# Fused sparse attention and spectral gate on one core: the POOL queue put in another order, with five smaller moves between engines

## The chip, the cores and the metric

The kernel runs on one core of a Trainium2 chip. A core has a matrix engine (PE, with weight loads shown apart as PEld), a vector engine (DVE), a scalar engine (ACT), a general engine (POOL) and SyncE (SP), which here only issues DMAs. Each engine works through its own instructions strictly in the order in which the program gave them, and waits on semaphores for the others. PE's results land in PSUM, everything else is kept in SBUF. The metric is the device time of one execution in microseconds (us), lower is better; a profiled execution also has a span, from its first to its last instruction.

## What is computed

First comes block-sparse attention: 4 batches of 8 heads, 768 positions, 64 wide, all float32. Each query sees its own block of 64 positions and, of the earlier blocks, those with the three best gate scores (its product with the mean key of a block); causal within that.

```python
k_rep = k.reshape(B, H, n_blocks, block, D).mean(axis=3)
gate_scores = np.einsum('bhsd,bhnd->bhsn', q, k_rep)
...
top_idx = np.argsort(gate_scores, axis=-1)[..., -top_k:]
...
mask = mask & (pos[:, None] >= pos[None, :])
scores = np.where(mask, scores, -1000000000.0)
...
return np.matmul(attn, v).astype(np.float32)
```

The heads of a batch, side by side, are the rows x (768 x 512) of a second stage, which multiplies a long convolution along the sequence with two gates:

```python
proj = x @ w_proj
...
X2 = np.fft.rfft(x2, n=S, axis=1)
H = np.fft.rfft(filter_fft, n=S, axis=0)[None, :, :]
x2_conv = np.fft.irfft(X2 * H, n=S, axis=1)
y = x1 * x2_conv * x3
return (y @ w_out).astype(np.float32)
```

## The kernel before

**Slots.** One loop runs over slots; slot number 3n + s is step s (0, 1, 2) of head n. In step s PE computes one third of head n's transposed scores (`scores`, L404: 4, 3 and 2 matmuls at L409 into a two-bank PSUM tile `sps`), ACT takes the exponential into one of four tiles `ex` (L412), and POOL clears what lies above the diagonal in place (`diagonals`, L415, called triangles below: two operations at L420 in step 0, one in steps 1 and 2). The product with the values follows one slot later (`product`, L426, matmuls L435 into `o`), at the end of PE's work of that slot; `normalise` (L445, DVE) and `turn_outputs` (L454) finish a head or a pair.

**Preparation.** Beside this, `prepare` makes head n+4 ready. In step 0 SP loads keys, queries and values of later heads; DVE casts the queries to fp16 (L306) and subtracts to get their rounding error `rem` (L308); POOL casts the keys (L299) and writes the scaled error (`low_query`, L311). The result `qk` has to be transposed into `qkT`. For heads below 12 (`PE_HEADS`) PE does it in step 2 (`turn_pe`, L329, copies by DVE and ACT at L331); from head 12 on SP issues a transposing DMA in step 1 (`turn_query`, L316). In step 1 of every even head, `gate` (L349 on PE, then DVE up to `gm`, L362) chooses the blocks of heads n+2 and n+3; the choice is transposed and put into `qkT` as 12 more rows, by PE and ACT below head 12 (L378, L380), by two rounds of DMAs on SP after that (`turn_mask`, L368, in step 2, then `place_mask`, L386, in step 0 of the next head). In step 2 POOL casts the values of head n+1 to fp16 (`cast_value`, L335). `prepare_first` has another order for heads 0 and 1, which have no lead of four heads.

**The second stage.** From head 9 on, each slot also holds one or no unit of the batch that has just been completed: X2 (L491, projections and their even and odd parts), F1 (L504, L507: forward transform; DVE multiplies with the filter's spectrum into four tiles `t`), X13 (L530: the two gates), F2 (L543, L546: inverse transform; ACT copies `yes`, DVE makes `yy`) and O (L565: output projection, ACT copies `osb`, SP stores). F1 and F2 stand in step 2 and leave a part for POOL, called in the next slot through the list `todo`: PQ (L519, L520, two subtractions and additions) after F1, yT (L557, L558, two products) after F2. With the plan written in the code these fall into step 0 of heads 11, 12, 13 (PQ) and 14, 15, 16, 17 (yT), and again 8 and 16 heads later; batch 3 follows the last head.

**The setup.** Before head 0, PE, DVE, POOL and ACT build a sine table FS (`phase_mm`, `phase_round`, `phase_turns`, `sines`; the phases are 128 x 384 PSUM tiles, two of them in the two banks of one tile), and head 0 and 1 are prepared; ACT's function table is loaded at its first instruction (L299), for the sines (L218) and for the exponential (L736). The filter is read in two halves `rows`, and in step 2 of heads 3, 4, 5 `filter_rows` turns the order of a block of its second half with a matmul (L624), copies it back on ACT (L625), and makes difference and sum on POOL (L626, L627); step 0 of heads 6, 7, 8 has the filter's spectrum (L635, L638). The weights come through 16 DMAs which POOL issues, 128 KB each (L664), in heads 3 to 13; they convert to fp16.

**What sets the order.** The program is scheduled by hand: the order of the calls in the loop is the order of the instructions on every engine, and nothing reorders them. In a slot it is: scores (with the exponential), normalise, turn_outputs, stores, prepare, diagonals, todo, setup, the unit, product of the slot before:

```python
        if n < NH:
            prepare(n, s)
            diagonals(n, s)
        for fn in todo:
            fn()
```

So in step 0 POOL's queue reads: cast of the keys, `low_query`, two triangles, PQ or yT; in step 2: cast of the values, one triangle.

Of the kernel before, what the change touches and what calls it, by code (L numbers as in the profile page):

```python
# [17 lines left out]
def kernel(  # L18
# [10 lines left out]
    nc = tc.nc  # L29

    B, H, S, D = q.shape
    P = 128
    SC = S // P
    NBLK = S // 64
    Dm = H * D
# [82 lines left out]
    for n in range(3):  # L118
        load_query(n)
        load_key(n)  # L120

# [68 lines left out]
    phases = {}  # L192

    def phase_mm(i):
        if i % 2 == 0:
            phases["big"] = big_tile("dftp")
        pr = phases["big"][:, 512 * (i % 2):512 * (i % 2) + F]
        nc.tensor.matmul(pr, lhsT=tvals[:, P * i:P * (i + 1)], rhs=fsin, start=True, stop=True)
        phases[i] = pr

# [99 lines left out]

    rems = {}

    def split_query(n, copy=nc.vector.tensor_copy):
        qk16 = qk16s[n % NB]
        q_nat = queries.pop(n)
        copy(qk16[:, 0, :, 0:D], q_nat)  # L306
        rems[n] = remp.tile([P, SC, D], FP32, name="rem", tag="rem")
        nc.vector.tensor_sub(rems[n], q_nat, qk16[:, 0, :, 0:D])  # L308

# [22 lines left out]

    def cast_value(n):
        vals[n] = v16s[n % NB]
        nc.gpsimd.tensor_copy(vals[n][:, :, 0:D], values.pop(n))  # L335

    GC = SC - 1

# [282 lines left out]
    def filter_rows(i):  # L621
        fa, fb = rows["all"][:, 0, i], rows["all"][:, 1, HC - 1 - i]
        rev = one_tile("rev")
        nc.tensor.matmul(rev, lhsT=flip, rhs=fb, start=True, stop=True)  # L624
        nc.scalar.copy(fb, rev)  # L625
        nc.gpsimd.tensor_sub(fil[:, 1, i, :], fa, fb)  # L626
        nc.gpsimd.tensor_add(fil[:, 0, i, :], fa, fb)  # L627

    spectra = {}

# [46 lines left out]
    for i in range(HC):  # L677
# [4 lines left out]
        at(7 + i, 0, spectrum_b, i)  # L682
        at(8 + i, 2, inverse_part, i, False)
        at(8 + i, 2, inverse_part, i, True)
    for i in range(DC):
        at(3 + i // 2, 1 + i % 2, weights, wp, moe_w_proj, slice(Dm, 2 * Dm), slice(i, i + 1))
        n = 5 + i
        at(n, 0, weights, wp, moe_w_proj, slice(P * i, P * (i + 1)), slice(0, DC))
        at(n, 1, weights, wp, moe_w_proj, slice(2 * Dm + P * i, 2 * Dm + P * (i + 1)), slice(0, DC))
        at(10 + i, 2, weights, wo, moe_w_out, slice(0, Dm), slice(i, i + 1))  # L690


    nc.vector.memset(lsc, 1.0)
# [27 lines left out]
    key_sums_mm(0, range(SC))  # L721
    small_constants(0)
    small_constants(1)
    turn_pe(0, 1, nc.scalar.copy)
    sines(0)
    key_sums_copy(0)
    key_sums_turn(0)
    turn_pe(0, 0, nc.scalar.copy)
    sines(1)
    key_sums_split(0)  # L730
    sines(2)
    split_query(1, nc.scalar.copy)
    turn_angles()
    nc.scalar.activation(tw, twf, AF.Sin, bias=0.0, scale=math.pi / S)

# [67 lines left out]
    def prepare_first(n, s):  # L803
        if (n, s) == (0, 0):
            gate([1])
            key_mask(2)
            ready_query(2)
            key_sums_mm(2, range(SC))
        elif (n, s) == (0, 1):
            turn_mask_pe([1])  # L810
            key_sums_copy(2)
            key_sums_turn(2)
            key_sums_split(2)
            turn_both(2)
            ready_query(3)
        elif (n, s) == (0, 2):
            turn_both(3)
            for i in range(1, NB):
                nc.gpsimd.memset(v16s[i][:, :, D:DV], 1.0)
            cast_value(1)  # L820
        elif (n, s) == (1, 0):
            gate([2, 3])
            ready_query(4)
        elif (n, s) == (1, 1):
            turn_both(4)
            nc.gpsimd.memset(flip16, 0.0)
            nc.gpsimd.affine_select(
                out=flip16, in_=flip16, compare_op=ALU.not_equal,
                fill=1.0, base=-(P - 1), pattern=[[1, P]], channel_multiplier=1)
            ready_query(5)  # L830
        else:
            turn_mask_pe([2, 3])
            turn_both(5)
            cast_value(2)
# [3 lines left out]
    for slot in range(max(units) + 1):  # L838
        n, s = divmod(slot, 3)
        todo, later = later, []  # L840
        if n < NH:
            if n % H == 0 and s == 0:
                xTs[n // H] = xtp.tile([P, DC, S], fp, name="xT", tag="xT")
            scores(n, s)
            if s == 2:
                scores_left[0] -= 1
        if s == 1 and 0 < n <= NH:
            normalise(n - 1)
        if s == 2 and n % 2 == 0 and 0 < n <= NH:
            turn_outputs(n // 2 - 1, xTs[(n - 1) // H])  # L850
        while stores and stores[0][0] <= slot - (2 if n < NH else 1):
            _, dst, osb = stores.pop(0)
            nc.sync.dma_start(dst, osb)
        if n < NH:
            prepare(n, s)
            diagonals(n, s)
        for fn in todo:
            fn()
        for fn, args in setup.get((n, s), []):
            fn(*args)  # L860
        for b, fn, *args in units.get(slot, []):
            if b not in stages:
                stages[b] = new_stage(b, xTs[b])
            act = fn(stages[b], *args)
            if act is not None:
                later.append(act)

        pn, ps = divmod(slot - 1, 3)
        if 0 <= pn < NH:
            product(pn, ps)  # L870
# [34 lines left out]
```

## Time and profile before

| what | value |
|---|---|
| runs shown | 304.82, 307.81, 309.74 us (median 307.81) |
| profiled execution | 304.75 us, span 303.0 us |
| PE busy (of the span) | 254.1 us (84%) |
| DVE busy | 202.7 us (67%) |
| POOL busy | 174.6 us (58%) |
| ACT busy | 170.7 us (56%) |
| mean granted PE clock | 0.961 |
| the chain that ended last | PE 51%, DVE 17%, POOL 11%, ACT 11%, nothing shown ("issue") 5% |
| start of the first scores | 16.7 us |

Times are counted from the first instruction. Durations below are of the profiled execution, which was the fastest of those shown. A row of the timeline reads: start, duration, engine, line, operation, out <- in, count, and in brackets the engine's idle time before it and what ended that. A row of the waits reads: who waited for whom, us in total, how often, and the longest. Matmuls overlap and their ends are modelled, so busy time of PE is not a measure of its peak.

### The profile page before, as it was taken

The page shows a single profiled execution, that of the slowest core. Times are in us where ns is not written, and L with a number is a line of the kernel's source. Part 1 is how long each engine was busy: PE and PEld are TensorE (multiplying, and loading weights), DVE is VectorE, ACT ScalarE, POOL GpSimd, SP SyncE. Part 2 cuts the span into 40 slices and gives each one's busy share as a digit, 9 for nine tenths or more (in the row PEclk, how much of TensorE's full clock was granted, in tenths as well). Part 3 has the DMA queues.
Part 4 walks back from the last instruction along what each step waited for, and adds up shares of the span by engine and source line. Part 5 has one row for each costly group of instructions (what it writes and reads, how often), then busy time and mean ns, then how long its engine had stood idle before and what let it go on. Part 6 is the DMA issues. An engine that isn't in the chain of part 4 may idle for free.

```text
span 303.0 us, 6290 instructions
## 1 busy us (share of the span) xinstructions
PE 254.1 (84%) x2221; PEld 149.6 (49%) x2221; DVE 202.7 (67%) x597; ACT 170.7 (56%) x254; POOL 174.6 (58%) x330
## 2 busy tenths in 40 slices
PE   5396876766778798888899889997999999999994
PEld 3264564544543355445645454565445565545541
DVE  6566376526898768966766888676588763479740
ACT  3745757365867435454655655576455668632363
POOL 7424557498675229867771386678524866517530
PEclk9999779599999969997999999999999999999999
DMA  9949936833369589898776888799739361000036
GB/s 171 214 90 276 188 80 121 157 45 47 36 78 186 119 148 195 132 201 154 160 148 129 205 160 176 148 206 194 162 77 176 84 94 71 35 35 2 0 144 238
DMA packets 127263, 40.03 MB, mean 132 GB/s; under 512 B 122128, under 2 KB 123392, under 8 KB 127232
## 3 DMA queue, kind: packets, MB, share of 16 engines
q1 hardware_dynamic: 121856, 37.54, 58.9%
q0 software_dynamic: 5376, 2.10, 6.7%
q8 instruction: 17, 0.28, 0.4%
q14 instruction: 14, 0.11, 0.2%
HBM read 24.64 MB, written 6.29 MB: 102 GB/s over the span
## 4 chain that ended last, share of the span: by engine, by line
PE 51%; DVE 17%; POOL 11%; ACT 11%; issue 5%; DMA 2%; SPq 0%; DVEq 0%; ACTq 0%; POOLq 0%
PE sps L409 8%; PE krp L267 7%; PE op L565 5%; PE o L435 5%; ACT ex L412 5%; POOL ex L420 4%; PE x13a L530 4%; PE x13b L530 3%; PE x2b L491 3%; PE x2a L491 3%; DVE rem L308 3%; PE tp L329 2%; POOL qk L311 2%; PE f2b L546 2%; ACT xT L463 2%
## 5 line engine op out<-in xcount | busy, mean ns | idle before, releaser
L412 ACT ACTIVATE ex<-sps 128x1024 f16<-128x1024 f32 (+2 forms) x96 | 87.7, 917 | 76.5 <-PE sps L409 67.9
L420 POOL TENSOR_SCALAR_AFFINE_SELECT ex<-ex 128x128 f16<-128x128 f16 (+1 forms) x128 | 45.0, 363 | 26.6 <-ACT ex L412 24.5
L409 PE MATMUL sps<-qkT 76*128 76x384 f16 (+2 forms) x288 | 55.6, 304 | 0.9 <-DMA qkT<-gmT 0.9
L435 PE MATMUL o<-v,ex 128*128 128x65 f16 x672 | 38.6, 198 | 20.9 <-POOL ex L420 19.1
L311 POOL TENSOR_SCALAR qk<-rem 128x384 f16<-128x384 f32 x32 | 16.8, 526 | 67.9 <-DVE rem L308 59.9
L435 PEld LDWEIGHTS <-ex 128*128 128x128 f16 x672 | 32.6, 100 | 41.3 <-POOL ex L420 26.3
L530 PEld LDWEIGHTS <-wp 128*128 128x128 f16 x256 | 25.1, 99 | 18.0 <-issue 3.5
L267 PE MATMUL krp<-k_nat,eblk 128*12 128x128 f32 (+2 forms) x144 | 28.4, 337 | 1.6 <-DMA k_nat<-in_k_dram 1.6
L409 PEld LDWEIGHTS <-qkT 76*128 76x128 f16 x288 | 21.4, 101 | 6.0 <-issue 1.1
L565 PE MATMUL op<-wo,yT 128*128 128x512 f16 x96 | 23.0, 379 | 0.0
L530 PE MATMUL x13a<-xT,wp 128*128 128x384 f16 x108 | 22.8, 334 | 0.2 <-DVE t L515 0.2
L535 DVE TENSOR_TENSOR gx<-x1sb,x13b 128x384 f32<-128x384 f16 x27 | 14.9, 552 | 12.0 <-ACT x1sb L534 6.5
L530 PE MATMUL x13b<-xT,wp 128*128 128x384 f16 x108 | 22.1, 327 | 0.2
L308 DVE TENSOR_TENSOR rem<-q_nat,qk 128x384 f32<-128x384 f32 x32 | 20.0, 625 | 3.3 <-ACT qk L306 1.0
L558 POOL TENSOR_TENSOR yT<-gx,yy 128x384 f16<-128x384 f32 x16 | 17.2, 1077 | 8.2 <-DVE yy L552 8.2
L519 POOL TENSOR_TENSOR PQ<-t,t 128x512 f16<-128x512 f32 x12 | 15.2, 1265 | 7.5 <-DVE t L512 7.5
L451 DVE TENSOR_TENSOR xn<-o,rz 128x384 f16<-128x384 f32 x32 | 17.8, 557 | 1.1
L329 PE MATMUL tp<-id_f,qk 128*76 128x128 f16 (+1 forms) x144 | 14.1, 252 | 4.4 <-POOL qk L311 2.8
L267 PEld LDWEIGHTS krp<-k_nat,eblk 128*12 128x12 f32 x144 | 11.8, 103 | 12.2 <-issue 4.3
L568 ACT COPY osb<-op 128x512 f32<-128x512 f32 x24 | 14.0, 585 | 6.2 <-PE op L565 5.4
L299 POOL CAST qk<-k_nat 128x384 f16<-128x384 f32 x31 | 16.8, 543 | 0.2
L335 POOL CAST v<-v_nat 128x384 f16<-128x384 f32 x32 | 16.3, 509 | 0.0
(134 smaller groups left out, 472.8 us busy)
## 6 DMA issues: line engine op xcount, KB each, us to landing
q_nat<-in_q_dram SPq DMA_DIRECT2D x32, 192.0 KB
k_nat<-in_k_dram SPq DMA_DIRECT2D x32, 192.0 KB
v_nat<-in_v_dram SPq DMA_DIRECT2D x32, 192.0 KB
out_dram<-osb SPq DMA_DIRECT2D x24, 256.0 KB
rows<-in_moe_filter_fft_dram SPq DMA_DIRECT2D x2, 768.0 KB
wp<-in_moe_w_proj_dram POOLq DMA_DIRECT2D x12, 128.0 KB, 3.5
wo<-in_moe_w_out_dram POOLq DMA_DIRECT2D x4, 128.0 KB, 4.1
qkT<-gmT SPq DMA_DIRECT2D x20, 18.0 KB
```

The source lines that it names most:

```text
L267: nc.tensor.matmul(sums[g][0:NBLK, 0:w * D], lhsT=eblk[:, c, :], rhs=keys[g][:, 0:w, c, :], start=(c == 0), stop=(c == SC - 1))
L308: nc.vector.tensor_sub(rems[n], q_nat, qk16[:, 0, :, 0:D])
L311: nc.gpsimd.tensor_scalar(qk16s[n % NB][:, 0, :, D:P], in0=rems.pop(n), scalar1=LO, scalar2=0.0, op0=ALU.mult, op1=ALU.add)
L329: nc.tensor.transpose(tp[0:rows_, P * c:P * (c + 1)], qk16s[n % NB][:, t, c, 0:rows_], id_f16)
L409: nc.tensor.matmul(sps[:, col:col + qe - qs], lhsT=turned[n][0:76, 1, kc, :], rhs=qT[0:76, qs:qe], start=True, stop=True, skip_group_check ...
L412: nc.scalar.activation(ex[:, lo:hi], sps[:, lo:hi], AF.Exp, bias=0.0, scale=scale)
L420: nc.gpsimd.affine_select(out=sub, in_=sub, compare_op=ALU.is_ge, fill=0.0, base=0, pattern=[[0, cnt], [1, P]], channel_multiplier=-1)
L435: nc.tensor.matmul(outs[n][:, qc * DE:(qc + 1) * DE], lhsT=ex[:, col + P * j:col + P * (j + 1)], rhs=vals[n][:, kc, 0:DE], start=(gi == 0 ...
L451: nc.vector.tensor_tensor(out=xns[n // 2][:, :, D * (n % 2):D * (n % 2 + 1)], in0=o[:, :, 0:D], in1=rz.to_broadcast([P, SC, D]), op=ALU.mult)
L491: nc.tensor.matmul(pp, lhsT=xT[:, dc, base + P * i:base + P * (i + 1)], rhs=wp[:, dc, Dm:2 * Dm], start=(dc == 0), stop=(dc == DC - 1))
L530: nc.tensor.matmul(dst, lhsT=wp[:, dc2, base:base + P], rhs=xT[:, dc2, hs:hs + HALF], start=(dc2 == 0), stop=(dc2 == DC - 1))
L565: nc.tensor.matmul(op, lhsT=yT[:, cc, P * scn:P * (scn + 1)], rhs=wo[:, cc, :], start=(cc == 0), stop=(cc == DC - 1))
```

## The change

Six things change. (1) The loop calls `prepare` after `diagonals` and `todo`, so POOL's queue in a slot holds the triangles first, then PQ or yT, then the casts and `low_query`; the instructions of the other engines keep their order by this, since `diagonals` and `todo` issue only to POOL while heads run. In `prepare_first`, heads 4 and 5 become ready one slot earlier on DVE and POOL (4 in slot (0, 2), 5 in (1, 1) ahead of the flip matrix), and head 4 is transposed in (1, 0). (2) From head 12 on ACT casts the values instead of POOL: 20 of the 32 casts. (3) `filter_rows` has no copy on ACT and nothing on POOL; DVE adds and subtracts straight out of PSUM. (4) The weights come in 8 DMAs of 256 KB in place of 16 of 128 KB. (5) ACT loads the sine table as its first table, so that the load between the first copy and the first sine is gone, and the first copies run under that table; ACT casts head 1's queries before the first sine instead of after the last. (6) The first two phases lie in the first banks of two PSUM tiles, the third in the second bank of the first tile. The program's instructions on PE are the same but for one exchange within slots (1, 0) and (1, 1); ACT has 20 casts more, 3 copies and one table load fewer; DVE has 6 operations more; POOL has 20 casts, 6 filter operations and 8 DMAs fewer, and SP's queue is unchanged.

```diff
--- before.py
+++ after.py
@@ -118,6 +118,7 @@
     for n in range(3):
         load_query(n)
         load_key(n)
+    nc.scalar.preload_act_table_set("trig_and_small")
 
 
 
@@ -192,9 +193,9 @@
     phases = {}
 
     def phase_mm(i):
-        if i % 2 == 0:
-            phases["big"] = big_tile("dftp")
-        pr = phases["big"][:, 512 * (i % 2):512 * (i % 2) + F]
+        if i < 2:
+            phases["big", i] = big_tile("dftp")
+        pr = phases["big", i % 2][:, 512 * (i // 2):512 * (i // 2) + F]
         nc.tensor.matmul(pr, lhsT=tvals[:, P * i:P * (i + 1)], rhs=fsin, start=True, stop=True)
         phases[i] = pr
 
@@ -300,10 +301,19 @@
 
     rems = {}
 
-    def split_query(n, copy=nc.vector.tensor_copy):
+    def split_query(n):
         qk16 = qk16s[n % NB]
         q_nat = queries.pop(n)
-        copy(qk16[:, 0, :, 0:D], q_nat)
+        nc.vector.tensor_copy(qk16[:, 0, :, 0:D], q_nat)
+        query_rest(n, q_nat)
+
+    def cast_query(n, copy):
+        copy(qk16s[n % NB][:, 0, :, 0:D], queries[n])
+
+    def query_rest(n, q_nat=None):
+        if q_nat is None:
+            q_nat = queries.pop(n)
+        qk16 = qk16s[n % NB]
         rems[n] = remp.tile([P, SC, D], FP32, name="rem", tag="rem")
         nc.vector.tensor_sub(rems[n], q_nat, qk16[:, 0, :, 0:D])
 
@@ -332,7 +342,8 @@
 
     def cast_value(n):
         vals[n] = v16s[n % NB]
-        nc.gpsimd.tensor_copy(vals[n][:, :, 0:D], values.pop(n))
+        copy = nc.gpsimd.tensor_copy if n < PE_HEADS else nc.scalar.copy
+        copy(vals[n][:, :, 0:D], values.pop(n))
 
     GC = SC - 1
 
@@ -622,9 +633,8 @@
         fa, fb = rows["all"][:, 0, i], rows["all"][:, 1, HC - 1 - i]
         rev = one_tile("rev")
         nc.tensor.matmul(rev, lhsT=flip, rhs=fb, start=True, stop=True)
-        nc.scalar.copy(fb, rev)
-        nc.gpsimd.tensor_sub(fil[:, 1, i, :], fa, fb)
-        nc.gpsimd.tensor_add(fil[:, 0, i, :], fa, fb)
+        nc.vector.tensor_add(fil[:, 0, i, :], fa, rev)
+        nc.vector.tensor_sub(fil[:, 1, i, :], fa, rev)
 
     spectra = {}
 
@@ -682,12 +692,13 @@
         at(7 + i, 0, spectrum_b, i)
         at(8 + i, 2, inverse_part, i, False)
         at(8 + i, 2, inverse_part, i, True)
-    for i in range(DC):
-        at(3 + i // 2, 1 + i % 2, weights, wp, moe_w_proj, slice(Dm, 2 * Dm), slice(i, i + 1))
-        n = 5 + i
-        at(n, 0, weights, wp, moe_w_proj, slice(P * i, P * (i + 1)), slice(0, DC))
-        at(n, 1, weights, wp, moe_w_proj, slice(2 * Dm + P * i, 2 * Dm + P * (i + 1)), slice(0, DC))
-        at(10 + i, 2, weights, wo, moe_w_out, slice(0, Dm), slice(i, i + 1))
+    for i in range(2):
+        half = slice(2 * i, 2 * i + 2)
+        at(3 + i, 1, weights, wp, moe_w_proj, slice(Dm, 2 * Dm), half)
+        at(5 + i, 0, weights, wp, moe_w_proj, slice(2 * P * i, 2 * P * (i + 1)), slice(0, DC))
+        at(5 + i, 2, weights, wp, moe_w_proj, slice(2 * Dm + 2 * P * i, 2 * Dm + 2 * P * (i + 1)),
+           slice(0, DC))
+        at(10 + i, 2, weights, wo, moe_w_out, slice(0, Dm), half)
 
 
     nc.vector.memset(lsc, 1.0)
@@ -721,15 +732,16 @@
     key_sums_mm(0, range(SC))
     small_constants(0)
     small_constants(1)
+    cast_query(1, nc.scalar.copy)
+    sines(0)
     turn_pe(0, 1, nc.scalar.copy)
-    sines(0)
     key_sums_copy(0)
     key_sums_turn(0)
     turn_pe(0, 0, nc.scalar.copy)
     sines(1)
     key_sums_split(0)
+    query_rest(1)
     sines(2)
-    split_query(1, nc.scalar.copy)
     turn_angles()
     nc.scalar.activation(tw, twf, AF.Sin, bias=0.0, scale=math.pi / S)
 
@@ -810,24 +822,24 @@
             turn_mask_pe([1])
             key_sums_copy(2)
             key_sums_turn(2)
+            turn_both(2)
             key_sums_split(2)
-            turn_both(2)
             ready_query(3)
+            for i in range(1, NB):
+                nc.gpsimd.memset(v16s[i][:, :, D:DV], 1.0)
         elif (n, s) == (0, 2):
             turn_both(3)
-            for i in range(1, NB):
-                nc.gpsimd.memset(v16s[i][:, :, D:DV], 1.0)
+            ready_query(4)
             cast_value(1)
         elif (n, s) == (1, 0):
             gate([2, 3])
-            ready_query(4)
+            turn_both(4)
         elif (n, s) == (1, 1):
-            turn_both(4)
+            ready_query(5)
             nc.gpsimd.memset(flip16, 0.0)
             nc.gpsimd.affine_select(
                 out=flip16, in_=flip16, compare_op=ALU.not_equal,
                 fill=1.0, base=-(P - 1), pattern=[[1, P]], channel_multiplier=1)
-            ready_query(5)
         else:
             turn_mask_pe([2, 3])
             turn_both(5)
@@ -852,10 +864,11 @@
             _, dst, osb = stores.pop(0)
             nc.sync.dma_start(dst, osb)
         if n < NH:
-            prepare(n, s)
             diagonals(n, s)
         for fn in todo:
             fn()
+        if n < NH:
+            prepare(n, s)
         for fn, args in setup.get((n, s), []):
             fn(*args)
         for b, fn, *args in units.get(slot, []):
```

## The prediction

> **What bounds the kernel now.** I read the page first. PE is busiest and heads the chain that ended last, but with half of it; DVE, POOL and ACT hold 39%. So PE is stopped by the others, and the question is where.
>
> ```profile
> PE 254.1 (84%) x2221; PEld 149.6 (49%) x2221; DVE 202.7 (67%) x597; ACT 170.7 (56%) x254; POOL 174.6 (58%) x330
> PEclk9999779599999969997999999999999999999999
> PE 51%; DVE 17%; POOL 11%; ACT 11%; issue 5%; DMA 2%; SPq 0%; DVEq 0%; ACTq 0%; POOLq 0%
> ```
>
> Second, the waits: PE (and its weight loads, in the same stalls) waits above all for POOL's triangles, and POOL above all for DVE's `rem`, although the triangles need no `rem`: `low_query` stands ahead of them in POOL's queue.
>
> ```profile
> POOL qk L311 <- DVE rem L308: 59.9, 24, 6.1
> PEld L435 <- POOL ex L420: 26.3, 24, 4.0
> PE o L435 <- POOL ex L420: 19.1, 16, 3.9
> ```
>
> Third, the timeline at the longest such stall, head 4. The first exponential ended at 50.50 (the merged row covers two).
>
> ```profile
> 49.48 1.83 ACT L412 ACTIVATE ex<-sps 128x1024 f16<-128x1024 f32 x2
> ...
> 50.66 1.38 POOL L627 TENSOR_TENSOR fil<-rows 128x512 f16<-128x512 f32 x1
> 51.02 1.43 DVE L308 TENSOR_TENSOR rem<-q_nat,qk 128x384 f32<-128x384 f32 x1
> 51.98 0.58 POOL L664 DMA_DIRECT2D wp<-in_moe_w_proj_dram  x1
> ...
> 53.17 0.51 POOL L311 TENSOR_SCALAR qk<-rem 128x384 f16<-128x384 f32 x1
> ...
> 53.75 1.01 POOL L420 TENSOR_SCALAR_AFFINE_SELECT ex<-ex 128x256 f16<-128x256 f16 x3
> ...
> 54.57 0.62 PE L435 MATMUL o<-v,ex 128*128 128x65 f16 x8 [3.94 <-POOL ex L420]
> ```
>
> Filter, weight DMA, cast and `low_query` all ran between the exponential and its triangle. Fourth, the same waits by stretch: PE waited for triangles 12.7 us from 16.7 to 111.0 (heads 0 to 10), 4.4 from 111.0 to 163.5, 2.0 after that. The loss is in the first third. Fifth, stretches at half the clock (columns: stretch, length, busy time of PE, PEld, DVE, ACT, POOL, then the clock):
>
> ```profile
> 40.28:43.69 3.41, 3.21 (x32) 2.79 (x30) 2.62 (x13) 2.36 (x4) 1.15 (x3) 0.50 0.51 115
> 53.93:60.76 6.83, 6.14 (x41) 4.19 (x42) 3.06 (x16) 2.95 (x5) 2.46 (x7) 0.50 0.90 173
> 105.13:111.96 6.83, 5.65 (x34) 3.37 (x35) 4.09 (x18) 1.56 (x3) 3.13 (x8) 0.50 0.73 125
> ```
>
> Two more are 30.04 to 33.45 (PE busy 3.27) and 139.27 to 142.68 (3.41). Each came after PE had stood 1.8 us or more: 2.25 at 27.5, 1.95 at 37.6, 3.94 at 50.6, 1.88 at 104.4, 1.80 at 135.3. Stalls of 2.47 at 63.0 and 2.05 at 87.2 had no such sequel, so the link isn't certain.
>
> **The change, part by part**, against the profiled execution (304.75 us, 3.06 below the median of the runs).
>
> *Start: −3.0.* The path was first copy (6.91 to 7.70), table load 1.28, sine, the second phase's addition, which waited 2.92 for that sine, the third, the cast of head 1 on ACT (11.47 to 11.97), `rem` (to 12.57), and only then the gate on DVE (12.48 to 14.53), scores at 16.71. Now: keys 0 are cast by 5.05, queries 1 (landed 5.42) by 5.95, sine 5.97 to 6.46, both copies to 8.66 (0.79 each, the first from 6.91). DVE has done its additions, key splits and `rem` (0.55 + 0.21 + 0.32 + 0.57 + 0.46 + 0.56 + 0.57 from 5.34) by 8.9. The gate starts near 9.1 instead of 12.48, which brings the exponential's table (two sines, 0.21, 1.28) in by 11.2 as the gate ends. That is 3.4 earlier; I take 3.0. Ends: 1.3, the table load's row alone, and 3.4.
> The row has no more than the load: 7.72 + 1.28, sine at 9.02. The Trainium skill, ScalarE: Activation LUTs, section "What ACT_TABLE_LOAD costs", counts a drain of 1380 ns with each switch, 2.66 us in all; by it this part would be 1.4 larger.
>
> *Triangles first, heads 1 to 10: −10.9.* A first triangle (both operations: 0.77) can now end 0.84 after its exponential. Heads 2, 4, 5, 8, 10: exponentials end at 37.42, 50.50, 62.07, 85.87, 103.79, triangles ended at 39.44, 54.51, 65.45, 89.20, 106.25; earlier by 1.18, 3.17, 2.54, 2.49, 1.62. Capped by the stalls (1.95, 3.94, 2.47, 2.05, 1.88) that is 1.18 + 3.17 + 2.47 + 2.05 + 1.62 = 10.49, and 0.39 at head 6.
> *Head 4 earlier: −2.3*, the 2.25 at 27.5 in which PE's transposes waited for `low_query` of head 4. Bounds 0 and 3.5 (with 0.54 and 0.71 at 23.7 and 33.8).
> *Filter on DVE: −1.9*, PE's wait of 1.94 at 69.9 for POOL's L627. DVE gets 6 operations; the nearest rows with an operand in PSUM and the same size are L495 and L496 (686, 679 ns): 4.1 us, hidden where DVE idles (60.0 to 68.6: busy 1.86 of 8.6). Without that cover they delay the next `rem`: at most +4.1.
> *What is late next.* Not all 15.1 stays: the second triangle still stands behind `low_query`, and in step 2 PE's transposes need it. In head 4 the first product ends at 52, scores and half the transposes at 52.8, and `low_query` at 53.2 or later: 0.4 to 1 returns. ACT's mask copies (two of 0.79 a pair) and DVE (14.57 busy in 17.9 from 84.2) come next. I keep two thirds: −10.1. Ends 5 and 15.1.
> *Clock: −4.* PE's 18.3 busy at half clock in the four stretches before 112 would take half at full, 9.1 less at most, 10.9 with the fifth. I take a bit under half, as other stalls remain; at the least 0.
>
> *Triangles first, heads 11 to 27: −3 +5 = +2.* These heads have PQ or yT in step 0. POOL's sum between the exponential and the second triangle is unchanged: 0.77 + 2.51 (PQ) + 0.51 + 0.51 = 4.3. Head 12: exponential ends 119.60, second triangle would end 124.25 instead of 124.40; the 1.05 won at the first product is lost at the second. With yT (1.9 to 2.0) head 14 keeps 1.0 of 1.80. Of 6.4 I keep 3.
> Against it, `low_query` itself comes later, and SP's transposes wait for it:
>
> ```profile
> 115.13 1.42 SPq L316 DMA_TRANSPOSE qkT<-qk  x1
> ...
> 120.18 0.40 PE L349 MATMUL gps<-kr,qkT 128*128 128x24 f16 x10
> ```
>
> In head 11 `low_query` ended at 114.23; now: 113.20 + 0.77 + 2.51 + 1.02 = 117.5. The transpose goes out at 117.5, 2.4 later, and lands (it took 3.84, to 118.97, by the trace's landing records) at 121.4; the gate used it at 120.18. In even heads the late transpose keeps SP from the mask's: head 12's L368 goes from 124.28 to about 125.5, and the mask's landing had 1.0 in hand. Going through all pairs by their slack at the old pace (odd heads 15, 19, 23, 27: 1.9, 1.65, 0.3, 0.8; masks for heads 14 to 30: 0.05 to 4.6) PE waits some 1.2, 0.65, 0.6, 0.3, 0.2 at gates and 2 at scores: 5. Ends 0 and, without slack, 9 odd heads at 2.4 and 8 even ones at 1.2: 31.
> A rule speaks against this order too. Row: `rem` takes 0.56, but 1.43 at 51.02, ending with POOL's L627. The Trainium skill, SBUF — State Buffer, section "SBUF: two separate sides", calls this an exclusive lock: a DVE operation with two SBUF inputs and a POOL operation exclude each other. Triangles used to follow `rem`; now they can meet it, at worst 0.56 in each of some 21 heads, 12 us by that rule.
>
> *Casts on ACT: 0.* 20 at 0.50 (L299 and L306 on ACT: 511, 502 ns), 10 us; ACT waits 67.9 us for PE before exponentials, 17.2 and 26.5 of it in the stretches concerned. Uncovered +10; POOL's 10 us less are a gain only through triangles, at best the 3 above again.
> *Weights: 0.* 16 issues of 0.73 and 0.61, 11.2 us of POOL, become 8; the 4-piece kind took 0.8, so 6.4 at most if the pieces set it (11.2 if bytes do). Triangles in front hide it. Ends −1 and +1.
>
> Sum: −3.0 − 10.1 − 4 + 2 = −15.1, 289.6. Runs scatter from 304.82 to 309.74, above the profiled one; I forecast **290**.
>
> **The rivals.**
> *The transposes become the bound.* For: slack of 0.05 to 1.9, and PE arrives earlier than before. Against: it only hits pairs with PQ or yT, and heads 18 and 26 recover. Without slack +31 against −3 − 10.1 − 4 − 3: 315.6, slower. It decides once the wait exceeds some 3 us for each of nine pairs. 7%.
> *The stall moves.* `low_query` and DVE stop PE in the early heads at another place and the clock stays as it was: −3 − 5 + 2, some 299. For: DVE is busy four fifths of the time from 84 on. Against: its waits for PE there. 15%.
> *ACT is late.* Casts uncovered, +10: 300. For: exponentials queue behind them. Against: the idle time named. 6%.
> *All of it is gained.* −3.0 − 15.1 − 10.9 − 3: 273. For: four of five slow-clock stretches follow a triangle stall. Against: it leaves PE almost no idle time. 10%.
> The forecast, 284 to 297, has 62%.
>
> **How the numbers follow.** The range 277 to 301 leaves out the slower case and the far end of the last. A measurement of this kernel tells about 2% from no change, so faster means below about 301. The forecast and the last case are faster; so is part of the 299 and 300 cases: 0.81. Same 0.10, slower 0.09.
>
> **What would show it.** First scores near 13.5; L311 waiting for `rem` no longer followed by PE's wait for L420 in heads 2 to 10; PE at L635 without a wait; no half clock at 40 and 54; L349 or L409 waiting for DMA `qkT` in heads 12 to 30; L412 not waiting behind casts. It would be wrong if PE's transposes (L329 before) wait for L311 as long as its products did, or if the gates wait more than 3 us a pair.

## The result and the profile after

The changed kernel takes **296.12 us** (median of 4 runs, 294.34 to 297.95); the kernel before, in runs beside it, 307.63. The ratio of times is **0.966, with a 95% interval of 0.956 to 0.975**: faster. The profiled execution of after is its slowest, 297.95 (span 296.2), and that of before its fastest, 304.75, so the traces differ by 6.8 us where the medians differ by 11.5. The four runs of after, 297.95, 296.55, 295.70 and 294.34, had mean clocks of 0.952, 0.965, 0.965 and 0.977: part of the scatter is how many stretches of half clock a run meets.

The page of after, its busy rows, the row of the granted clock, and the shares of the chain that ended last:

```profile
PE 253.3 (86%) x2221; PEld 147.7 (50%) x2221; DVE 201.7 (68%) x603; ACT 175.5 (59%) x270; POOL 160.7 (54%) x296
PEclk9797999999799958999999999978999999999999
PE 51%; DVE 16%; POOL 10%; ACT 8%; DMA 7%; issue 5%; SPq 1%; POOLq 0%; DVEq 0%; ACTq 0%
```

The chain has a little less of POOL and ACT, and DMA has grown from 2% to 7%. The waits of after answer to those of before (us in total, times, longest):

```profile
POOL ex L431 <- ACT ex L423: 93.4, 50, 5.1
...
PEld L446 <- POOL ex L431: 10.0, 15, 1.2
...
PE o L446 <- POOL ex L431: 7.9, 12, 1.1
...
PE sps L420 <- DMA qkT<-gmT: 6.0, 3, 2.9
...
POOL qk L321 <- DVE rem L318: 4.7, 5, 2.2
...
PE gps L360 <- DMA qkT<-qk: 2.9, 3, 1.8
```

POOL's wait for `rem` fell from 59.9 to 4.7 us, and POOL now idles where its triangles wait for ACT's exponentials, which is harmless. PE's wait for triangles fell from 19.1 to 7.9. PE now waits 8.9 us for DMAs into `qkT`, against 0.9 before. The timeline of after at head 4, where the longest stall was:

```profile
43.39 1.83 ACT L423 ACTIVATE ex<-sps 128x1024 f16<-128x1024 f32 x2 [0.89 <-PE sps L420]
...
44.48 0.89 POOL L431 TENSOR_SCALAR_AFFINE_SELECT ex<-ex 128x256 f16<-128x256 f16 x2 [1.34 <-ACT ex L423]
...
45.21 0.57 DVE L318 TENSOR_TENSOR rem<-q_nat,qk 128x384 f32<-128x384 f32 x1
...
45.43 0.42 PE L446 MATMUL o<-v,ex 128*128 128x65 f16 x8 [0.32 <-POOL ex L431]
...
46.24 0.50 POOL L321 TENSOR_SCALAR qk<-rem 128x384 f16<-128x384 f32 x1
```

The triangles start as the first exponential ends, nothing stands between, and the product waits 0.32 us instead of 3.94. Now the same two stretches in both kernels, from the first scores of head 0 to those of head 11, and from there to head 31 (columns: stretch, length, busy time of PE, PEld, DVE, ACT, POOL with the number of instructions, clock, DMA share, GB/s). Before:

```profile
16.71:110.97 94.26, 72.25 (x718) 45.74 (x716) 61.99 (x213) 56.68 (x76) 53.65 (x106) 0.90 0.64 117
110.97:254.60 143.63, 130.25 (x1187) 74.71 (x1184) 104.01 (x302) 84.49 (x128) 92.95 (x172) 0.98 0.78 155
```

After:

```profile
12.96:93.98 81.02, 67.33 (x717) 41.78 (x716) 64.02 (x218) 54.79 (x73) 45.08 (x95) 0.94 0.73 141
93.98:247.78 153.80, 135.28 (x1188) 77.53 (x1185) 101.31 (x303) 92.12 (x148) 88.16 (x152) 0.94 0.71 148
```

This is the whole account. The start is 3.75 shorter (16.71 to 12.96). Heads 0 to 10 lost 13.24: PE idles 13.7 instead of 22.0, and its same matmuls take 67.3 instead of 72.3, since less of them runs at half clock. Heads 11 to 30 gained 10.17: PE idles 18.5 instead of 13.4, and its matmuls take 5.0 longer, at a clock of 0.94 instead of 0.98. From head 31 on nothing changed (48.4 in both). −3.75 − 13.24 + 10.17 is −6.8, the difference of the two profiled executions.

So the early heads gave about what was forecast, and three quarters of it (10.2 of 13.2) were given back later in this trace. PE's waits for `qkT` from DMAs in after, all of them after head 11's start:

```profile
102.76 0.61 PE L420 MATMUL sps<-qkT 76*128 76x128 f16 x4 [1.66 <-DMA qkT<-gmT]
108.45 0.31 PE L360 MATMUL gps<-kr,qkT 128*128 128x24 f16 x5 [1.85 <-DMA qkT<-qk]
136.19 0.61 PE L420 MATMUL sps<-qkT 76*128 76x128 f16 x4 [1.44 <-DMA qkT<-gmT]
169.19 0.29 PE L360 MATMUL gps<-kr,qkT 128*128 128x24 f16 x5 [0.54 <-DMA qkT<-qk]
197.40 1.03 PE L420 MATMUL sps<-qkT 76*128 76x128 f16 x4 [2.90 <-DMA qkT<-gmT]
232.77 0.29 PE L360 MATMUL gps<-kr,qkT 128*128 128x24 f16 x5 [0.52 <-DMA qkT<-qk]
```

Before had one of 0.90. The first two and the 2.90 lie in or just before the two late stretches of half clock:

```profile
103.80:114.04 10.24, 8.39 (x58) 4.77 (x56) 4.81 (x20) 3.95 (x7) 4.78 (x8) 0.50 0.95 183
195.96:202.79 6.83, 5.39 (x33) 3.06 (x34) 2.52 (x7) 2.12 (x3) 3.13 (x5) 0.50 0.77 150
```

### The profile page after: what moved, and what is told of

It reads as the page before. It is cut to its first block, busy times and chain, and to the rows that moved or that the text cites. A ratio compares the mean times of both kernels' runs of the same rounds, so it can differ in the third digit from the quotient of the medians.

```text
span 296.2 us, 6301 instructions
## 1 busy us (share of the span) xinstructions
PE 253.3 (86%) x2221; PEld 147.7 (50%) x2221; DVE 201.7 (68%) x603; ACT 175.5 (59%) x270; POOL 160.7 (54%) x296
## 4 chain that ended last, share of the span: by engine, by line
PE 51%; DVE 16%; POOL 10%; ACT 8%; DMA 7%; issue 5%; SPq 1%; POOLq 0%; DVEq 0%; ACTq 0%
PE sps L420 7%; PE op L576 6%; PE krp L268 6%; DMA qkT<-qk 6%; PE x13b L541 5%; ACT ex L423 4%; PE o L446 4%; PE x2a L502 4%; PE x13a L541 4%; PE x2b L502 3%; POOL ex L431 3%; PE tp L339 2%; PE f1b L518 2%; ACT osb L579 1%; POOL qk L321 1%
## 5 line engine op out<-in xcount | busy, mean ns | idle before, releaser
L423 ACT ACTIVATE ex<-sps 128x1024 f16<-128x1024 f32 (+2 forms) x96 | 87.4, 917 | 67.3 <-PE sps L420 64.1
L431 POOL TENSOR_SCALAR_AFFINE_SELECT ex<-ex 128x128 f16<-128x128 f16 (+1 forms) x128 | 50.4, 408 | 98.3 <-ACT ex L423 93.4
L446 PEld LDWEIGHTS <-ex 128*128 128x128 f16 x672 | 33.0, 99 | 26.0 <-POOL ex L431 10.0
L446 PE MATMUL o<-v,ex 128*128 128x65 f16 x672 | 38.7, 196 | 7.9 <-POOL ex L431 7.9
L268 PE MATMUL krp<-k_nat,eblk 128*12 128x128 f32 (+2 forms) x144 | 27.7, 327 | 1.9 <-POOL dft_ka L210 1.9
L541 PE MATMUL x13b<-xT,wp 128*128 128x384 f16 x108 | 23.3, 341 | 0.5 <-DVE t L526 0.3
L318 DVE TENSOR_TENSOR rem<-q_nat,qk 128x384 f32<-128x384 f32 x32 | 19.1, 598 | 3.2 <-POOL qk L321 0.5
L339 PE MATMUL tp<-id_f,qk 128*76 128x128 f16 (+1 forms) x144 | 13.4, 246 | 5.2 <-POOL qk L321 1.9
L268 PEld LDWEIGHTS krp<-k_nat,eblk 128*12 128x12 f32 x144 | 11.0, 98 | 12.9 <-issue 5.2
L506 DVE TENSOR_TENSOR x2eo<-x2a,x2b 128x512 f16<-128x512 f32 x11 | 7.6, 687 | 11.9 <-PE x2b L502 11.9
```

The lines of the kernel that those rows point to most:

```text
L268: nc.tensor.matmul(sums[g][0:NBLK, 0:w * D], lhsT=eblk[:, c, :], rhs=keys[g][:, 0:w, c, :], start=(c == 0), stop=(c == SC - 1))
L339: nc.tensor.transpose(tp[0:rows_, P * c:P * (c + 1)], qk16s[n % NB][:, t, c, 0:rows_], id_f16)
L423: nc.scalar.activation(ex[:, lo:hi], sps[:, lo:hi], AF.Exp, bias=0.0, scale=scale)
L431: nc.gpsimd.affine_select(out=sub, in_=sub, compare_op=ALU.is_ge, fill=0.0, base=0, pattern=[[0, cnt], [1, P]], channel_multiplier=-1)
L446: nc.tensor.matmul(outs[n][:, qc * DE:(qc + 1) * DE], lhsT=ex[:, col + P * j:col + P * (j + 1)], rhs=vals[n][:, kc, 0:DE], start=(gi == 0 ...
L541: nc.tensor.matmul(dst, lhsT=wp[:, dc2, base:base + P], rhs=xT[:, dc2, hs:hs + HALF], start=(dc2 == 0), stop=(dc2 == DC - 1))
```

## The experiments

Two questions were open. What lengthens the late heads: `low_query` behind PQ and yT, the casts on ACT, or something else? And which part earns the early gain? All diffs are against the changed kernel unless the text says before. The columns: first scores of head 0, heads 0 to 10 (to the first scores of head 11), heads 11 to 30, all from one trace; then the ratio of run times to the kernel before, measured beside it, with its interval; then the range of the run times, with the traced one. No stage times are given for e8, e10 and e11: their traces are of 291.63, 299.08 and 291.91 us, where their runs start at 286.31, 294.02 and 287.32.

| kernel | start | heads 0–10 | heads 11–30 | ratio (95%) | runs, us (traced) |
|---|---|---|---|---|---|
| before | 16.7 | 94.3 | 143.6 | 1 | 304.82–309.74 (304.75) |
| after | 13.0 | 81.0 | 153.8 | 0.966 (0.956–0.975) | 294.34–297.95 (297.95) |
| e1 old order from head 11 | 13.1 | 79.8 | 147.6 | 0.954 (0.950–0.959) | 289.27–291.00 (290.59) |
| e2 casts between triangles and PQ | 12.9 | 81.6 | 144.1 | 0.949 (0.942–0.956) | 287.16–293.19 (288.69) |
| e3 all values cast on POOL | 12.9 | 82.1 | 150.2 | 0.971 (0.962–0.979) | 293.18–296.73 (295.31) |
| e4 before + order alone | 16.6 | 91.8 | 153.6 | 1.019 (1.011–1.027) | 308.55–312.11 (312.11) |
| e5 filter back on ACT and POOL | 13.1 | 86.6 | 150.4 | 0.990 (0.982–0.998) | 300.17–303.63 (300.17) |
| e6 all but the order | 13.1 | 89.8 | 146.1 | 0.972 (0.962–0.982) | 295.57–301.32 (299.15) |
| e7 old start | 16.3 | 79.8 | 150.0 | 0.972 (0.963–0.980) | 296.20–302.54 (296.20) |
| e9 old `prepare_first` | 13.2 | 85.4 | 151.1 | 0.979 (0.971–0.988) | 296.58–299.85 (299.85) |
| e12 before + order, `prepare_first`, filter | 16.5 | 81.3 | 147.9 | 0.978 (0.965–0.990) | 295.82–304.16 (295.82) |

How far apart two traces of the same instructions can lie, the table shows itself. After, e1, e2 and e3 have the same program up to head 10, and take 79.8 to 82.1 there. After, e3, e4, e5, e7, e9 and e12 have the same order in the late heads, and take 147.9 to 153.8 there. So the late loss against before is 4 to 10 us, and the trace of after is at the top of this; differences of 2 us early and of several late tell nothing by themselves.

### The late heads

**e1: from head 11 on, the order of before.**

```diff
         if n < NH:
+            if 11 <= n < NH:
+                prepare(n, s)
             diagonals(n, s)
...
-        if n < NH:
+        if n < 11:
             prepare(n, s)
```

> The changed kernel, but from head 11 on prepare is called ahead of the triangles again, as in the kernel before. Theory A (the late low_query makes PE wait for SP's transposes in heads 11 to 30; the gain is all in the start and heads 1 to 10): PE's waits for DMA at L349 and L409 (9.0 us in the changed kernel) fall below 2 us, heads 11 to 31 take about 152 us instead of 160, and the time is 288 to 291. Rival B (ACT's value casts or the meeting of triangles and DVE's rem cost the time in the later heads, the DMA waits only show it): 294 to 297, since the casts stay on ACT and POOL's waits for rem come back.

Median 290.50. The late heads take 147.6 instead of 153.8, PE's waits for DMA fall from 8.9 to 3.2 us, and the early gain stays. So the order in the late heads is what gives most of the gain back, 6.2 of the 10.2 in these two traces. All its runs are below those of after. Of the 4.0 that stay against before, 2.4 is idle time of PE and 1.6 the clock; the waits at head 12 (below) are 3.0.

**e2: `prepare` between the triangles and PQ or yT, in all heads.**

```diff
         if n < NH:
             diagonals(n, s)
+            prepare(n, s)
         for fn in todo:
             fn()
-        if n < NH:
-            prepare(n, s)
```

> The changed kernel with the order triangles, prepare, todo: the triangles stay first, and the casts and low_query go ahead of PQ and yT. Theory A: low_query ends 2.0 to 2.5 us earlier in heads 11 to 17, 19 to 25 and 27, the DMA waits at L349 and L409 fall from 9.0 to under 3 us, the half clock near 104 and 196 us is gone, and the time is 284 to 290, below the first of these runs, since the triangles keep their place. Rival B: 293 to 297. If PQ and yT, now behind low_query's wait for rem, come late for F2 and O, PE waits at L557 or L576 and the time stays near 296.

Median 289.26, ratio 0.949, 1.8% below the change itself. The two intervals just touch, but no run of e2 (at most 293.19) is as slow as the fastest of after (294.34), so this version beats both kernels. The late heads take 144.1, as in before, with the early gain kept. The wait rows of e2 (whole run):

```profile
PE o L446 <- POOL ex L431: 7.9, 12, 1.1
...
PE sps L420 <- DMA qkT<-gmT: 2.5, 2, 1.7
...
PE gps L360 <- DMA qkT<-qk: 1.3, 1, 1.3
```

The triangles cost PE the same 7.9 as in after; only the DMA waits went. How, is seen at head 22. POOL and SP in the timeline of after (head 22 starts at 181.68, head 23 at 188.08):

```profile
185.49 0.99 POOL L569 TENSOR_TENSOR yT<-gx,yy 128x384 f16<-128x384 f32 x1
...
187.11 0.51 POOL L321 TENSOR_SCALAR qk<-rem 128x384 f16<-128x384 f32 x1
...
187.65 1.43 SPq L326 DMA_TRANSPOSE qkT<-qk  x1
...
190.08 1.26 SPq L379 DMA_TRANSPOSE gmT<-gm  x1
...
193.84 1.96 SPq L397 DMA_DIRECT2D qkT<-gmT  x2
```

and in e2 (starts at 177.81 and 184.19):

```profile
181.22 0.51 POOL L321 TENSOR_SCALAR qk<-rem 128x384 f16<-128x384 f32 x1
...
181.76 1.43 SPq L326 DMA_TRANSPOSE qkT<-qk  x1
...
184.22 1.25 SPq L379 DMA_TRANSPOSE gmT<-gm  x1
...
187.95 1.94 SPq L397 DMA_DIRECT2D qkT<-gmT  x2
```

In after `low_query` ends 5.9 us after its head's start, behind yT; SP's transpose follows at once, the mask's transpose stands behind it in SP's queue, then `place_mask`: 5.76 after the start of head 23. In e2 `low_query` ends at 3.9 and the masks are placed 3.76 after head 23's start, 2.0 sooner. Head 24 needs them: it waits 2.90 in after (197.40), 0.80 in e2.

One pair of waits stayed: at the first scores of head 12 and at its gate, 1.98 and 1.05 in e1, 1.69 and 1.29 in e2, where after has 1.66 and 1.85. There `low_query` isn't the cause. In after it ends at 100.49, but SP is still issuing `place_mask` (99.70 to 101.45), and the transpose goes out at 101.56, 7.58 us after head 11's start. In e2 `low_query` ends 2.46 us closer to the start, and the transpose goes out at 7.60 all the same. From 92 to 103 SP issues with no gap over 0.21, with the two transposes of the filter's tables (L236, L238, 2.5 us) among its work. PE reaches head 11 17.0 us sooner than before (110.97 to 93.98), SP this transpose only 13.6 sooner (115.13 to 101.56).

**e3: all values cast on POOL**, in after; **e8:** the same in e2.

```diff
-        copy = nc.gpsimd.tensor_copy if n < PE_HEADS else nc.scalar.copy
+        copy = nc.gpsimd.tensor_copy
```

> The changed kernel with all values cast on POOL. Theory A: the casts on ACT are hidden and POOL's cast stands in step 2 behind the triangle, where POOL has room: 295 to 298, with the same DMA waits of about 9 us. Rival B (ACT's 20 casts of 0.5 us delay the exponentials): 287 to 292.

> e2_casts_before_pq (289.3: triangles, prepare, PQ or yT) with all values cast on POOL. Theory A (the casts are hidden on ACT, and on POOL they stand behind a triangle in step 2): 288 to 292, no difference that can be told. Rival B (ACT's casts delay exponentials or the copies behind them): 284 to 287, with heads 11 to 31 taking 2 to 4 us less than 144.

e3: 295.57, ratio 0.971 against 0.966 of after; e8: 290.07, 0.939 (0.928 to 0.949) against 0.949 of e2. Neither differs measurably from its partner, and PE's DMA waits in e3 are 6.9. So the casts on ACT are neither a cost nor a gain beyond the 1% or so that the intervals leave open.

**e11: e2 with PQ and yT held back one slot** (all but the last PQ of a batch).

```diff
             diagonals(n, s)
+            prepare(n, s)
+        if s == 0 and n < NH and n % H != 5:
+            todo, later = [], todo
```

> e2_casts_before_pq with PQ and yT held back for one more slot, behind the second triangle, except the last PQ of a batch. Theory A (what PE still loses to triangles in heads 11 to 27 is PQ or yT between the first and the second triangle): waits of PE for L431 after head 11 fall from 5.5 us to under 2, heads 11 to 31 take 140 to 142 us instead of 144, the time is 284 to 288. Rival B (PE waits for something else as soon as it is earlier: masks, transposes, ACT): 288 to 291 with the wait shifted to DMA qkT or ACT.

Median 289.18, ratio 0.948: no different from e2. The waits of e11, in its trace of 291.91 us, say why:

```profile
PE sps L420 <- DMA qkT<-gmT: 6.6, 4, 3.0
...
PE o L446 <- POOL ex L431: 3.3, 5, 1.1
...
PE x13a L541 <- DVE t L526: 1.9, 2, 1.3
...
PE x13b L541 <- DVE t L526: 1.5, 3, 0.8
```

PE's late waits for triangles went from 5.4 us in e2 to 0.8, but waits for placed masks came, 6.6, and 3.4 for DVE's `t`, whose tiles PQ empties. With POOL out of the way the chain of the masks ends last there, as rival B said. That this trace stands for the other runs of e11 isn't shown.

### The early heads

**e4: before, with the new order in the loop and nothing else.**

```diff
--- before
         if n < NH:
-            prepare(n, s)
             diagonals(n, s)
         for fn in todo:
             fn()
+        if n < NH:
+            prepare(n, s)
```

> The kernel before with the loop's order alone (triangles, todo, prepare; nothing else). Theory A: the start stays at 16.7 us, heads 1 to 10 win some 8 us, heads 11 to 31 lose 5 to 8 to waits for transposes: 299 to 306, a small gain or none. Rival B (the order itself is all gain, other parts take it back): 292 to 297.

Both expectations missed: 309.55, ratio 1.019, slower than before. Heads 0 to 10 gain 2.5 (PE idles 3.5 less, its matmuls take 1.0 longer), and the late heads lose 10, as in after. Two things in its trace. First, head 4:

```profile
51.55 1.83 ACT L412 ACTIVATE ex<-sps 128x1024 f16<-128x1024 f32 x2
...
52.74 1.37 POOL L627 TENSOR_TENSOR fil<-rows 128x512 f16<-128x512 f32 x1
...
53.10 1.43 DVE L308 TENSOR_TENSOR rem<-q_nat,qk 128x384 f32<-128x384 f32 x1
...
54.06 0.58 POOL L664 DMA_DIRECT2D wp<-in_moe_w_proj_dram  x1
...
54.65 0.78 POOL L420 TENSOR_SCALAR_AFFINE_SELECT ex<-ex 128x256 f16<-128x256 f16 x2
...
55.48 0.42 PE L435 MATMUL o<-v,ex 128*128 128x65 f16 x8 [2.78 <-POOL ex L420]
```

The cast and `low_query` are gone from the gap, but the filter and the weight DMA of the slot before still stand between exponential and triangle. Second, a stretch at half clock, five times 3.41 us long:

```profile
29.20:46.30 17.10, 14.76 (x122) 10.71 (x123) 9.63 (x42) 9.24 (x12) 7.27 (x17) 0.50 0.61 142
```

PE had waited 1.54 us, until 30.22, for head 4's `low_query`. What such a stretch costs, e9 tells below.

**e9: after, with `prepare_first` of before** (head 4 ready in (1, 0) and transposed in (1, 1), head 5 after the flip matrix; two small moves in slots (0, 1) and (0, 2) go back with it).

```diff
...
         elif (n, s) == (0, 2):
             turn_both(3)
-            ready_query(4)
             cast_value(1)
         elif (n, s) == (1, 0):
             gate([2, 3])
-            turn_both(4)
+            ready_query(4)
         elif (n, s) == (1, 1):
-            ready_query(5)
+            turn_both(4)
...
```

> The changed kernel with prepare_first of before: heads 4 and 5 become ready one slot later. Theory A (under the new order of the loop, the casts of head 4 stand behind two triangles in slot (1, 0) and PE's transposes need them one slot later, as the order alone showed with 1.54 and 0.72 of waits there and 17 us at half clock after it): head 2 starts at 33 to 35 instead of 31.2, and the time is 298 to 301. Rival B (the other parts carry it): head 2 at 31 to 32 and 295 to 297.

Median 297.84, ratio 0.979, an interval that overlaps that of after. In its trace heads 0 to 10 take 4.4 longer. The same stall as in e4 is there, and the same slow stretch behind it (rows of PE's timeline for the queries of heads 3 and 4, then the stretch, two windows out of it, and heads 0 to 10):

```profile
21.18 0.51 PE L339 MATMUL tp<-id_f,qk 128*128 128x128 f16 x6 [1.01 <-POOL qk L321]
...
26.86 0.82 PE L339 MATMUL tp<-id_f,qk 128*128 128x128 f16 x6 [1.54 <-POOL qk L321]
```

```profile
26.30:43.40 17.10, 15.21 (x123) 10.76 (x123) 9.22 (x40) 9.66 (x13) 7.58 (x18) 0.50 0.59 135
33.13:36.54 3.41, 3.41 (x35) 2.08 (x32) 1.60 (x6) 1.36 (x2) 0.41 (x2) 0.50 0.39 88
36.54:39.96 3.42, 2.81 (x31) 2.21 (x28) 3.21 (x20) 2.25 (x4) 2.38 (x6) 0.50 0.25 58
13.23:98.62 85.39, 72.57 (x717) 45.18 (x716) 63.77 (x218) 54.89 (x73) 44.13 (x95) 0.88 0.69 133
```

After has its stall one head earlier, at the queries of head 3:

```profile
21.77 0.76 PE L339 MATMUL tp<-id_f,qk 128*128 128x128 f16 x6 [1.86 <-POOL qk L321]
```

So preparing head 4 sooner moved the wait for `low_query` from head 4 (1.54, after 1.01 at head 3) to head 3 (1.86). PE idles no less in after, 13.7 us in heads 0 to 10 against 12.8 in e9; all of the 4.4, and 0.9 more, is the clock, 72.6 us of busy PE against 67.3 for the same instructions. The mean clocks of e9's runs went from 0.945 to 0.971, so not each of them need have met this stretch, and that this part pays over the runs isn't shown.

**e5: the filter back on ACT and POOL.**

```diff
-        nc.vector.tensor_add(fil[:, 0, i, :], fa, rev)
-        nc.vector.tensor_sub(fil[:, 1, i, :], fa, rev)
+        nc.scalar.copy(fb, rev)
+        nc.gpsimd.tensor_sub(fil[:, 1, i, :], fa, fb)
+        nc.gpsimd.tensor_add(fil[:, 0, i, :], fa, fb)
```

> The changed kernel with the filter as before: copied back on ACT, subtracted and added on POOL. Theory A (in heads 4 to 6 the filter's 2.6 us on POOL stand ahead of the next triangles, whatever the loop's order, as the order alone still waited 2.8 and 1.8 us at heads 4 and 5): PE waits some 2 to 3 us for L431 in heads 4 and 5 and 1.9 for fil in head 6, head 10 starts at 92 to 95 instead of 88.0, and the time is 299 to 303. Rival B (the fold saves the one wait at the spectrum): 297 to 298, head 10 at 90.

Median 302.75, ratio 0.990, clear of after's interval. Heads 0 to 10 take 5.6 longer, 2.1 of it idle time of PE (15.8 against 13.7), the rest the clock. PE's waits for triangles rise again and the wait for `fil` is back:

```profile
PE o L446 <- POOL ex L431: 10.5, 11, 2.5
...
PE hspa L646 <- POOL fil L638: 1.9, 1, 1.9
```

The longest, 2.51, is at head 4, 1.24 at head 5: the stall seen in e4. The fold is what makes "triangles first" true in the slots after a filter block.

**e6: all but the order in the loop.**

```diff
         if n < NH:
+            prepare(n, s)
             diagonals(n, s)
...
-        if n < NH:
-            prepare(n, s)
```

> The changed kernel with the loop's order of before (prepare ahead of the triangles in all slots); the other five parts and the order inside prepare_first stay. It differs from e1_old_from_11 (290.5) in heads 0 to 10 alone. Theory A (triangles first wins there what the waits for L420 were, less what comes back): 8 to 10 us of waits for triangles in heads 1 to 10 return, head 10 starts at 94 to 98 and the time is 297 to 301. Rival B (the early gain is the filter, the weights and the start, and the order does nothing, as the order alone left head 10 at 102.3): head 10 starts at 87 to 90 and the time is 289 to 292.

Median 298.83, ratio 0.972. Heads 0 to 10 take 8.8 longer than in after (idle time of PE 16.3 against 13.7, the rest the clock), and `PE o L446` waits 17.5 us for triangles instead of 7.9; the late heads are 7.7 shorter, with DMA waits of 0.5. Over the whole kernel the order, as it is made, gains 0.7% on top of the other parts, less than the intervals tell.

**e12: before with order, `prepare_first` and filter fold**; start, weights and casts as before.

> The kernel before with three of the parts: the loop's order, prepare_first, the filter on DVE. Theory A (these three make the early gain together, the order alone made none): heads 1 to 10 take 75 to 77 us (85.4 before, 85.7 with the order alone), head 10 starts at 91 to 94, and the time is 298 to 302. Rival B (weights and ACT's casts are needed as well): head 10 at 96 or later, 303 to 308.

Median 300.58, ratio 0.978. Heads 0 to 10 take 81.3 in its trace (of 295.82 us, where its runs go up to 304.16): with these three alone the early gain can be complete. Against after it then lacks the start, 16.5 against 13.0; the two ratios overlap.

### The start and the weights

**e7: the start undone** (sine table loaded at first use, first two phases in one tile, queries of head 1 cast on ACT after the last sine).

```diff
-    nc.scalar.preload_act_table_set("trig_and_small")
...
-        if i < 2:
-            phases["big", i] = big_tile("dftp")
-        pr = phases["big", i % 2][:, 512 * (i // 2):512 * (i // 2) + F]
+        if i % 2 == 0:
+            phases["big"] = big_tile("dftp")
+        pr = phases["big"][:, 512 * (i % 2):512 * (i % 2) + F]
...
```

> The changed kernel with the start of before: the sine table loaded between the first copy and the first sine, two phases in one tile, head 1's queries cast last. Theory A (the start is on the path and its gain stays): first scores at 16.6 instead of 13.0, time 299 to 301. Rival B (a later wait absorbs it): first scores at 16.6, but head 10 at 88 to 89 and 295 to 297.

The first scores move from 12.96 to 16.30, as before; at head 11 2.1 of these 3.3 are left. Median 298.25, ratio 0.972 against 0.966, a difference inside the intervals.

**e10: 16 weight DMAs.**

```diff
+    for i in range(DC):
+        at(3 + i // 2, 1 + i % 2, weights, wp, moe_w_proj, slice(Dm, 2 * Dm), slice(i, i + 1))
+        n = 5 + i
...
```

> The changed kernel with 16 weight DMAs of 128 KB. Theory A (POOL has room for 5 us more in heads 3 to 13 now that triangles go first): 295 to 298, head 10 at 88 to 89. Rival B (POOL's issues stand between triangles as the filter did, 0.6 to 0.8 each): head 10 at 90 to 92 and 298 to 301.

Median 298.15, ratio 0.972 (0.959 to 0.984), which holds the ratio of after. This doesn't tell the two apart; what the weights are worth stays open, within some 1%.

## Why the prediction was right, and where not

The direction was right, and 296.12 lies in the range of 277 to 301. The gain was smaller than forecast: 11.5 us between the medians where 290 meant 17.6, and 6.8 between the traces where the sum said 15.1. The early terms held and one late term failed, by 8 us; that the total still fell into the range is in part luck, since the range was wide. By its own steps, in the two traces:

- **Start, −3.0: −3.75.** The working gave 3.4. The sine table now loads at 0.80, far from the path, and the two first copies run under it. The gate starts 2.98 earlier (9.50); most of the rest is a gate of 1.55 us on DVE instead of 2.05, which the working didn't have. In the run times e7 doesn't tell the start from nothing.
- **Heads 1 to 10, −10.1, and clock, −4: −13.2 together**, to head 11's start. The windows split it: 8.3 less idle, 4.9 less busy. The half-clock stretches at 40 and 54 went, as said (three of 3.41 us, near 12, 22 and 76, are left). By PE's waits, triangles gave 10.3 (12.7 to 2.4) of the 10.9 and the filter its 1.9, but `low_query` only 0.9 (2.8 to 1.9) of the 2.3 for head 4, since that wait moved to head 3. Of these 13.1 other waits took back 4.8 (the largest new one 1.78 at 74.33, for DVE's `xn`); the step that keeps two thirds had this about right. What failed is the pricing part by part. The order had 10.9, but alone (e4) it brought 2.5; taken out of the whole, the order costs 8.8, the filter 5.6 and the preparation 4.4, more than the 13.2 they gain, and most of these costs is clock. Order and filter aren't terms of a sum but conditions of one gain: either left out leaves stalls of 2.0 to 2.5 at PE (e6, e5). For the preparation of head 4 this isn't shown. The prediction's head 4 row had the filter and the weight DMA in the gap, yet let the order clear it.
- **Heads 11 to 27, −3 + 5 = +2: +10.2** (4 to 10 by the traces with the same late order). This term failed on size. Of the 3 to be gained at triangles, 0.9 came (PE waited 6.4 before, 5.5 after, in heads 11 to 30): the stall moved to the second triangle more fully than thought. The DMA waits, forecast as 5, rose by 8.0 (0.9 to 8.9). And a term was missing: the half clock around these waits. PE's matmuls take 5.0 longer, with the stretches at 103.8 and 196.0; in e1 and e2, where the wait at head 24's scores (2.90 in after) is gone and 0.80, there is no stretch near it. e1 and e2 confirm the mechanism and add to it that the waits at head 12 come with SP's full queue, not from `low_query`. The clock step as a whole, early and late, is then about 0 instead of −4.
- **The lock between DVE and POOL.** Triangles are slower behind the new order: their mean rose from 363 to 408 ns, 5.4 us over 128 of them, where the prediction's worst case had 12; with the old order put back (e6) it is 366. That each delay is a meeting with `rem` isn't shown. `rem` itself fell from 625 to 598 ns, and took 1.43 us beside the filter again in e4 (53.10). It ends 0.42 after L627 there, and 0.41 after it in before, not with it, as the prediction read the row.
- **Filter.** DVE's six operations took 681 and 678 ns, priced at 686 and 679; PE's wait for `fil` is gone.
- **Casts, 0:** 20 at 518 ns, hidden (e3, e8). **Weights, 0:** 8 issues of 829 and 780 ns, 6.6 us of POOL instead of 11.3: twice the bytes took 0.10 and 0.17 us more an issue. e10 leaves their worth open.
- **The rivals.** "The transposes become the bound" came true in part: 8.9 us of waits, far from the 31. "The stall moves" was wrong for most of the early heads (idle time and half clock fell) and right for `low_query` there and for the late ones. "ACT is late" has nothing for it (e3, e8), and "all of it is gained" missed by 23 us.

The Trainium skill, ScalarE: Activation LUTs, section "What ACT_TABLE_LOAD costs", counts a drain of 1380 ns with each switch of tables. The trace of after doesn't show one: `tw` ends at 9.92, the exponential's table loads at 9.93 and takes 1.28.

## What to carry to other kernels

In an in-order queue, put the work that others are about to wait for first, but order the rest by who waits as well: `low_query` belonged behind the triangles and ahead of PQ and yT (e2), since SP's DMAs with little slack hang on it. Price a stall by the instructions that stand in the gap, all of them: while one remains, removing the others gains little, and the parts of such a change have no prices of their own. A stall moved to another place isn't a stall saved (head 4's to head 3). Where an engine arrives sooner, look at the queue that doesn't: a DMA queue that issues without gaps keeps its pace.

## What the runs showed of the hardware

Short stalls of PE were followed by long stretches at half clock, with PE busy in them. In e4 and e9 one wait of 1.54 us went over into 17.10 us at 0.50, with PE busy for 14.76 and 15.21 of it; in after 10.24 us with 8.39 busy. Not every stall had such a sequel: 1.44 us at 136.19 in after had none. The lengths 6.83, 10.24 and 17.10 are two, three and five times 3.41 to within 0.05. The Trainium skill, TensorE: Matmul & The Clock Gate, section "What's actually happening", has the clock return to full after one busy window of about 3.4 us; in e9 the window from 33.13 to 36.54 is busy throughout by the records (3.41), and the next is at half clock all the same. The measurement decides; what in these stretches kept the clock low, their short gaps or the kind of their instructions, isn't settled by these runs. The stretches aren't a fixed property of the code either: four runs of the same kernel had mean clocks from 0.952 to 0.977.

A transposing DMA on SP isn't quick or even: its issue alone took from 1.39 to 2.28 us in after, and the one issued at 101.56 landed 6.85 us later.
